# A new stored order for a gated-attention and MLP kernel, and a last result that leaves in thirds

## The chip, the cores and the metric

The kernel runs on one core of a Trainium2 chip. The metric is the device time of one execution in microseconds, lower is better: 575.98 us is the median of three runs, 575.77 to 577.02. Engines are named as in the profile: PE is TensorE, PEld its weight loads, DVE VectorE, ACT ScalarE, POOL GpSimd, SP SyncE, which here issues the DMAs.

## The reference

Gated linear attention with a complex gate over 4 × 8 heads, 768 steps, head dimension 48, and on its output an MLP of width 384 → 2048 → 384 over 3072 tokens:

```python
mag = np.sqrt(a_re * a_re + a_im * a_im)
scale = np.minimum(mag, 0.999) / (mag + 1e-06)
a_re_n, a_im_n = (a_re * scale, a_im * scale)
for t in range(S):
    new_re = ar * S_re - ai * S_im
    new_im = ar * S_im + ai * S_re
    kv = np.einsum('bhd,bhe->bhde', k[:, :, t], v[:, :, t])
    S_re, S_im = (new_re + kv, new_im)
    y[:, :, t] = np.einsum('bhd,bhde->bhe', q[:, :, t], S_re)
...
h = x @ w_in
g = h * (1.0 / (1.0 + np.exp(-1.702 * h)))
return (g @ w_out).astype(np.float32)
```

## The kernel before

**Attention.** The recurrence is turned into masked products. For each unit of 256 steps, VectorE and ScalarE make from the gate `ri` its magnitude and angle: squares (helper L253), their sum (L270), logarithm and exponential (L365, L366, L374 to L377), the scaled gate (L367) and its clipped magnitude (L380), the angle (L385). Scans along time (L390, L406, L424) give running products and running angles; cosine and sine (L443, L444) turn the queries and keys, and the rotated ones are `qr` and `qk` (all tensor products of two operands have the helper's line L270). Five DMAs on SP then lay each of them out by head in `qkh` (L466, L467, L469, the "remap"). Unit 0 is cut into two parts of 128 steps so that TensorE may start early. `attend` computes for each block of 128 steps and half of the heads the scores (L504), their masking (L508, `pm`), the mixing with the values and the state (L529), the transposed keys (L560, in `kz_ps`; evicted to `kt` by ScalarE at L563 or by VectorE at L564) and the state's update (L554, L569, L573). `kz_ps` holds one pair of transposed heads, so the next transposition waits for the eviction.

**MLP.** The weights come as 16 tiles (A0 to A7 of w_in, U0 to U7 of w_out) of 64-bit words from DRAM into one of four `raw` tiles (L286); ScalarE scales the low words (L288), VectorE takes the top words in two steps (L289, L292) and adds the low ones (L295). The first two blocks, of 256 tokens each, use the fp32 tiles as they are; for the five later ones, of 512 tokens, weights, tokens and hidden values are split into a high and a low part (L304, L307 for weights; `gh` and `gl`, L627 and L629). L610 is the hidden product, L619 and L623 the gating function, L643 the projection, L659 the eviction of the three 128×512 result tiles `o`, L664 the result DMA.

**Order.** All of this is added to one plan of 1827 steps with declared reads and writes. `Plan.order` decodes a table of step numbers (`ORDER`) and a set of steps that run on their second engine (`OTHER`), and the steps are then written out in that order under a manual schedule; so each engine's queue, and SP's, is the table's. The durations given with each step were used only to make the table. A table load (L840) is put ahead of each ScalarE function that needs another set of functions. L451 is a row of matmuls without use for the result, put ahead of the first real ones and between them.

Of the kernel before, what the change touches and what calls it, by code (L numbers as in the profile page):

```python
# [105 lines left out]
}  # L106
ORDER = (
    "0D=He00jUK0A&EF0001&0D}O808#*j08s#j08;>m00#h60EhsK00;n80E_@x09F7701*I>09pWD0FVF)09ycF0Eqxx0AT=%09OE!09XKL0Ac`N"
    "0Av9W0AK(L02u&{0B8V?0FwY|0097M0F(f10A>LQ0Brzk00ID&0SN$-0B-<e0SW+a0B``B0C50w0Gj}o0CE8l0Gt4U0CWJD0TKY60GR-F0G<F0"
    "02%;x00RJ@0Cxcs01E(k0HOe(00aRP0C@nT0Sf^P0HFXB02=`f0Hgq>01yDB0H**P0Tloe0T}?Q0H^^L0I~oR0T%#z0UZFd0T=+Z01W{i0DAzn"  # L110
    "0DJ(y0U7|S0JZ@i0IUFg0Ji}k02TnQ0IdMH0UH2*01g1J0J#9L0UQA+03HB;0I>kN0J{LZ0U-e?0Kfnh0LTD<0LcKs0VM$=03!jm0KEXh0U`jt"
    "0LlQv0K@>x0386u0LB3%04)Ka0L%c#0L}o^0M7sy0V)970M-B`02lz;03QG#04M=003`t60Ve@103iU?0VV+0044y}0Neq%03ra{04@PA05SmG"
    "0k;6q04D)40O0`Q04V`405<^M0V@FG0L=k10WJV4051UF0l5G$0lEO~04o8z0OSEP05bu<0W<*R05||S0W|<D0OkRl0lWdg06YOU0PFxd0OtTP"
    "0O$e306_sb0O|ng06PJ}05k!X0P6w50mK0g0mlH*0Pg_q0MY@y0P+Ae0m%Um0Mh_I0Qmqm0lon90muQx0m=c(080VJ0Pq1#07e1+06hTl0QCXR"
    "0YL#d0YU+u0Yd>g0Qdn!06zgY0Y?El0Q3Mu0nY(F0XzWu0Yv~n0Zsu(073yt0nh;U0ZIWz0nz|O0QUjY0nGtR07U^l0Y3rJ0ZakR0agLt0YCu$"
    "0Z#x-0oDOm0Z;+e0RREl0h$3=0RI3;0oVXX0Z{>207(I?0a5{40n`9Z0aE}<0aOA108Rk=0bBu90Q>=60RaL40cipO0onor0b&8!0owut0b>E&"
    "0tf;G0bT)U0hj^?08au30Q~`%0to^P0RjRJ0tEpB0crvY0hs}G0t*5S0bc<G0c8ON0uTXj0b~IN0uKQP0cHVP0ulkL0u%vf0ipsI0c!zZ0p9`i"
    "0;U2H0q6o40pI~_0uupl0bv1c0vQ2z0dN8p0viE!0u}-30vrK)0vZ8#0v`dc0o?(z0e}J^0v-Wz0v!Qz0k8rg0;d9~0doPg0ek|f0eAu<0;&Qe"
    "0qO#)0pS7b0pkL&0pbDf0wMwI0<i()0;~b$0wn?O0rdf!0<Hn@0eJ$l0i6P`0<!|N0e%630qp{{0=5Br0iOc60gM5C0=EHy0p<d_0p|hn0fz#u"
    "0>1+L0fqs80rmpG0igl%0=WVC0ww~y0rLU(0x$vi0fYiE0=of&0x|+80r~<n0{jBO0s8_p0z3iy0yY7S0sR6u0w@890>c5L0fhp@0=)r=0g3|s"  # L120
# [20 lines left out]
    "1+WDq2E+xq2E_!B1u+K31tkT#1?&Yg1d#=<1d;`@1u_LU2FC`-1d|5I1+N9|1-k`31vCY`1vLfl1vUjd2FeD@1vm!G1@Q&+1v&*j1vv%11wRF{"
    "2F(V}1-}LE1x5zX1waMx1v>>u1wjVT1;7RM1;GZ<1w;k*2GRw>1wsWw1yBV^1@i^?1xE(c2Gj-j1-=H=1^NX_1+xW31xp3;1^ES11^fk02G$1G"
    "1^Wir1e66)1xy7~1x*G31;YhZ1_1@M1^ouu1+@m+1-1s;1;z!p1<wUf1zH7G2HXbS1yly!1;qvg1^xxN1zQDN1;+)@1;hnc1y}`N1!V<Y1zrXJ"
    "1<?lI1!M-`2H^$*1z81V1=0m>1z-i!1;_=}1<3_s1z`o$1!)H21=a;)1!o511!xB31#ksy1<D5H1!@Kb2Id881<MBK1<VC;1#$(~1#bn|2IvL`"
    "1#Ja$2I&Us1=$7%1{wwq1_%Xt1`h?z1=<Gd1<nTS1$YJn2JHqA1_=fc1_}le2JQwM1#|}Q1`7u81{4Mi1$G5`1`P%k1{?)-1{MW<1|0?y2Jr?L"
# [869 lines left out]
```

## Time and profile before

| | before |
|---|---|
| median of three runs | 575.98 us |
| profiled execution | 577.74 us, of which the span in the trace 576.0 us |
| mean granted clock of TensorE | 0.993 |
| TensorE matmuls busy | 535.9 us (93%), 6236 matmuls |
| VectorE busy | 453.5 us (79%) |
| ScalarE busy | 312.9 us (54%) |
| SP's DMA queue | 79.09 MB, 50.7% of 16 engines |

TensorE is the busiest engine by the mean, but the mean lies over three stages: a start in which TensorE has hardly work, a long stretch in which it has no idle time, and an end in which the last results leave. Each is to be read apart.

### The profile page before, as it was taken

To read this page: it belongs to the slowest core of one execution; us is meant where nothing else is said; L and a number is where in the kernel's file an instruction comes from. 1 tells how busy PE (TensorE), PEld (TensorE's weight loads), DVE (VectorE), ACT (ScalarE), POOL (GpSimd) and SP (SyncE) were. 2 spreads that over 40 slices of the span, in tenths; PEclk is the share of its full clock that TensorE was granted. 3 is DMA by queue.
4 is the path that set the end of the run, shared out by engine and by line. 5 is a ranking of instruction groups with operands and counts; after the bars stand their busy time and mean duration, and the time that the engine had idled before them with its cause. 6 is when DMAs were issued, how large, how long until landed. Compare 5 with 4: busy or idle time off the path is not lost.

```text
span 576.0 us, 14758 instructions
## 1 busy us (share of the span) xinstructions
PE 535.9 (93%) x6236; PEld 444.4 (77%) x6236; DVE 453.5 (79%) x822; ACT 312.9 (54%) x458; POOL 27.0 (5%) x86
## 2 busy tenths in 40 slices
...
GB/s 302 219 142 292 200 202 308 82 189 100 159 87 193 56 166 145 124 122 166 138 185 69 123 165 180 73 225 92 92 140 57 191 127 85 58 55 56 37 93 66
DMA packets 30902, 80.06 MB, mean 139 GB/s; under 512 B 4208, under 2 KB 7024, under 8 KB 30832
## 3 DMA queue, kind: packets, MB, share of 16 engines
q1 hardware_dynamic: 30832, 79.09, 50.7%
...
q14 instruction: 21, 0.17, 0.1%
HBM read 55.44 MB, written 4.72 MB: 104 GB/s over the span
## 4 chain that ended last, share of the span: by engine, by line
PE 84%; DVE 9%; DMA 2%; ACT 1%; issue 1%; SPq 1%; POOL 0%; DVEq 0%; POOLq 0%
PE o_ps L643 33%; PE h_ps L610 33%; PE x_ps L529 6%; PE p_ps L504 5%; PE kz_ps L560 4%; PE kz_ps L554 2%; DMA raw<-in_w_in_dram 1%; DMA qkh<-qr 1%; DVE valA L292 1%; DVE s L406 1%; DVE pm L508 1%; PE h_ps L451 1%; DVE qr L270 1%; DVE qk L270 1%; DVE valU L295 1%
## 5 line engine op out<-in xcount | busy, mean ns | idle before, releaser
L623 ACT ACTIVATE g<-h_ps 128x512 f32<-128x512 f32 x80 | 46.4, 596 | 121.7 <-PE h_ps L610 85.2
L643 PE MATMUL o_ps<-gh,hiU 128*128 128x512 f32 x240 | 95.7, 399 | 0.0
L610 PE MATMUL h_ps<-xhi,hiA 128*128 128x512 f32 x240 | 95.4, 398 | 0.0
L643 PE MATMUL o_ps<-gl,hiU 128*128 128x512 f32 x240 | 93.7, 391 | 0.0
L610 PE MATMUL h_ps<-xhi,loA 128*128 128x512 f32 x240 | 93.6, 390 | 0.0
L643 PE MATMUL o_ps<-gh,loU 128*128 128x512 f32 x240 | 93.5, 390 | 0.0
L610 PE MATMUL h_ps<-xlo,hiA 128*128 128x512 f32 x240 | 93.4, 389 | 0.0
L840 ACT ACT_TABLE_LOAD x61 | 78.3, 1283 | 1.9 <-PEq L1003 0.8
L627 DVE CAST gh<-g 128x512 fp32r<-128x512 f32 x74 | 31.0, 421 | 42.8 <-PE o_ps L643 26.1
L629 DVE TENSOR_TENSOR gl<-g,gh 128x512 fp32r<-128x512 f32 x80 | 54.6, 684 | 2.4 <-ACT gh L626 0.7
L677 DVE TENSOR_REDUCE fit<-raw_w 128x1 f32<-128x256 f32 x96 | 38.0, 413 | 19.0 <-DMA raw_w<-in_w_out_dram 17.5
L643 PEld LDWEIGHTS o_ps<-gl,hiU 128*128 128x128 f32 x240 | 45.1, 188 | 9.9 <-DVE gl L629 0.4
L610 PEld LDWEIGHTS h_ps<-xhi,loA 128*128 128x128 f32 x240 | 45.1, 188 | 9.6
L643 PEld LDWEIGHTS o_ps<-gh,hiU 128*128 128x128 f32 x240 | 45.1, 188 | 9.1 <-issue 0.4
L610 PEld LDWEIGHTS h_ps<-xlo,hiA 128*128 128x128 f32 x240 | 45.1, 188 | 8.8
L643 PEld LDWEIGHTS o_ps<-gh,loU 128*128 128x128 f32 x240 | 45.1, 188 | 8.7
L610 PEld LDWEIGHTS h_ps<-xhi,hiA 128*128 128x128 f32 x240 | 45.1, 188 | 8.6
L563 ACT ACTIVATE kt<-kz_ps 128x224 f32<-128x224 f32 x66 | 23.3, 353 | 46.1 <-PE kz_ps L560 34.0
L643 PE MATMUL o_ps<-g,valU 128*128 128x256 f32 x192 | 44.8, 380 | 1.7 <-ACT g L619 1.7
L270 DVE TENSOR_TENSOR qk<-qk,s 128x768 f32<-128x768 f32 (+1 forms) x52 | 45.6, 888 | 0.5 <-DMA qk<-in_qk_dram 0.4
L508 DVE TENSOR_TENSOR pm<-p_ps,mask 128x512 f32<-128x512 f32 x48 | 32.8, 683 | 15.1 <-PE p_ps L504 12.3
L610 PE MATMUL h_ps<-x,valA 128*128 128x256 f32 x192 | 44.2, 381 | 0.0
...
## 6 DMA issues: line engine op xcount, KB each, us to landing
...
```

The source lines that it names most:

```text
L270: add(en, t, rank, lambda: e.tensor_tensor(out=out, in0=a, in1=b, op=alu), **kw)
L504: mm(p_ps[to : to + QL, j, lo:L], lhsT=at(h, 1, c)[:, lo : lo + QL], rhs=at(h, 0, c)[:, lo:L], start=True, stop=True)
L508: add("DVE", d_t(CW), rk(4 * c + hh), lambda hh=hh: dve.tensor_tensor(out=pm[hh], in0=p_ps, in1=mask, op=ALU.mult), r=["P"], w=[f"pm{hh}"])
L529: mm(x_ps[32 * j : 32 * j + 32, r, :], lhsT=lt, rhs=rt, start=n == 0, stop=n == len(steps) - 1)
L563: one = ("ACT", a_t(2 * KD) - 0.12, lambda e=e: act(out=kt[0][:, 2 * e : 2 * e + 2, :], in_=k_ps, func=AF.Copy))
L610: mm(h_ps[hb][:, hs], lhsT=ww[:, r * T + f * P : r * T + (f + 1) * P], rhs=x[:, r, :], start=r + k == 0, stop=r == NR - 1 and k == len(ter ...
L623: add("ACT", a_t(N) - 0.15, rk(i + f / 2), lambda hb=hb, hs=hs: act(out=g32[hb][:, hs], in_=h_ps[hb][:, hs], func=AF.Silu, scale=SLOPE), r ...
L627: two = ("DVE", d_t(N, 2), lambda hb=hb, hs=hs: dve.tensor_copy(out=high.g(hb)[:, hs], in_=g32[hb][:, hs]))
L629: add("DVE", d_t(N), rk(i + f / 2), lambda hb=hb, hs=hs: dve.tensor_tensor(out=glo[hb][:, hs], in0=g32[hb][:, hs], in1=high.g(hb)[:, hs].b ...
L643: mm(o_ps[m][:, 0:N], lhsT=y[:, f * DM + m * P : f * DM + (m + 1) * P], rhs=x[:, hs], start=i == 0 and f == 0 and k == 0, stop=i == NP - 1 ...
L677: add("DVE", d_t(CK), rk + 2, lambda x=x, op=op: dve.tensor_reduce(out=f_w[:, x, n : n + 1], in_=weights.looked_at()[:, :, 1], op=op, axis ...
L840: nc.scalar.preload_act_table_set(o[5])
```

## The change

Three things are changed. The table `ORDER` and the set `OTHER` are new. Of the steps with two engines, 34 have changed theirs: of the K evictions ten go to ScalarE (L563) and two to VectorE; of the weight splits three to ScalarE and two to VectorE; single squares, conversions, evictions and lines go either way, and the last of the three final result evictions goes to ScalarE. The table loads on ScalarE are 63 instead of 61; the matmuls are the same 6236.

The durations that the planner was given for a weight load, a load of queries and keys and a load of values are changed; they act only where a table is made. And in the last block the eviction and the DMA of each third no longer depend on the other users of the tile that they write.

```diff
-        add("SP", 1.9 + 1.3 * (n == 0), rk - 4, lambda: dma(out=raw.bitcast(I32), in_=(w_in if m == "A" else w_out)[j].bitcast(I32)),
+        add("SP", 1.9, rk - 4, lambda: dma(out=raw.bitcast(I32), in_=(w_in if m == "A" else w_out)[j].bitcast(I32)),
...
-        add("SP", z * (1.9 if np_ == 2 else 1.0), rk("ldqk"), lambda: dma(
+        add("SP", z * 1.5, rk("ldqk"), lambda: dma(
...
-            add("SP", 0.87, rk(4 * c) - 5, lambda vt=vt, c=c: dma(out=vt, in_=v[u, c]), w=[kv])
+            add("SP", 1.04, rk(4 * c) - 5, lambda vt=vt, c=c: dma(out=vt, in_=v[u, c]), w=[kv])
...
-            either("D", one, two, rk(NP + 0.1), r=[f"o{m}"], w=[f"ob{m}"] + spent)
+            either("A" if final and m == NR - 1 else "D", one, two, rk(NP + 0.1), r=[f"o{m}"], w=[f"ob{m}"] + ([] if final else spent))
         for ms in (((0,), (1,), (2,)) if final else ((0, 1, 2),)):
             add("SP", len(ms) * N * P * 4 / 410e3, rk(NP + 0.1), lambda ms=ms: dma(
                 out=to[:, ms[0] : ms[-1] + 1, :], in_=high.o(n)[:, ms[0] : ms[-1] + 1, 0:N]
-            ), r=[f"ob{m}" for m in ms] + spent)
+            ), r=[f"ob{m}" for m in ms] + ([] if final else spent))
```

The first rows in which VectorE's queue differs, at the start of the program, before (`valA` is a weight tile, `s` are the gate's factors, `ri` the gate):

```order
L270 TENSOR_TENSOR s_80<-s_80,s_81 128x3x128 x2
L289 TENSOR_SCALAR valA_149<-raw_72 128x768
L367 SCALAR_TENSOR_TENSOR s_81<-ri,s_80 128x3x128
L292 SCALAR_TENSOR_TENSOR valA_149<-raw_72,valA_149 128x768
L367 SCALAR_TENSOR_TENSOR s_81<-ri,s_80 128x3x128
L289 TENSOR_SCALAR valA_160<-raw_74 128x768
L380 TENSOR_SCALAR s_80<-s_80 128x3x128 x2
```

and in the changed kernel:

```order
L270 TENSOR_TENSOR s_80<-s_80,s_81 128x3x128 x2
L367 SCALAR_TENSOR_TENSOR s_81<-ri,s_80 128x3x128
L380 TENSOR_SCALAR s_80<-s_80 128x3x128
L289 TENSOR_SCALAR valA_152<-raw_72 128x768
L367 SCALAR_TENSOR_TENSOR s_81<-ri,s_80 128x3x128
L292 SCALAR_TENSOR_TENSOR valA_152<-raw_72,valA_152 128x768
L380 TENSOR_SCALAR s_80<-s_80 128x3x128
L295 ISA valA_152<-raw_72,valA_152 128x1536
```

One scaled gate and one clipped magnitude now stand ahead of the first step that needs a weight tile. Further down the same queue, the rows that stand ahead of the first rotated queries (`qr`), before:

```order
L289 TENSOR_SCALAR valA_208<-raw_71 128x768
L270 TENSOR_TENSOR qr<-qk,s_80 128x3x128 x2
L424 SCALAR_TENSOR_TENSOR s_85<-small,s_81 128x128 x3
L270 TENSOR_TENSOR qk<-qk,s_85 128x3x128
L406 SCALAR_TENSOR_TENSOR s_84<-s_80,small,s_82 128x128 x3
```

and in the changed kernel:

```order
L289 TENSOR_SCALAR valA_207<-raw_74 128x768
L437 TENSOR_SCALAR small<-s_85 128x3
L398 TENSOR_SCALAR small<-s_83 128x3
L399 RECIPROCAL small<-small 128x3
L424 SCALAR_TENSOR_TENSOR s_85<-small,s_81 128x128 x3
L406 SCALAR_TENSOR_TENSOR s_84<-s_80,small,s_82 128x128 x3
L270 TENSOR_TENSOR qr<-qk,s_80 128x3x128 x2
```

The scans of part 1 (L424, L406) stand ahead of the queries of part 0 instead of behind them. ScalarE's queue at the first evictions of K (`kt`), before:

```order
L365 ACTIVATE s_82<-s_82,small 128x3x256
L288 ACTIVATE raw_74<-raw_74 128x768
L366 ACTIVATE s_82<-s_82 128x3x256
L376 ACTIVATE s_83<-s_82,small 128x3x256
L374 ACTIVATE s_81<-s_81,small 128x3x256
L563 ACTIVATE kt_97<-kz_ps 128x224
```

and in the changed kernel:

```order
L365 ACTIVATE s_82<-s_82,small 128x3x256
L366 ACTIVATE s_82<-s_82 128x3x256
L376 ACTIVATE s_83<-s_82,small 128x3x256
L563 ACTIVATE kt_97<-kz_ps 128x224 x2
L288 ACTIVATE raw_74<-raw_74 128x768
```

The first two evictions stand ahead of L374, which needs VectorE's L367. The end of SP's queue, as a difference (`o` holds the last results, the names behind "waits" are the engines waited for):

```order
 L695 DMA raw_w<-in_a_dram 128x256 [waits DMAHW2_49,DVE_49]
-L664 DMA out_dram<-o_5701 128x512 [waits DVE_49]
-L664 DMA out_dram<-o_5701 128x512 x2
+L664 DMA out_dram<-o_5703 128x512 [waits DVE_49] x2
+L664 DMA out_dram<-o_5703 128x512 [waits Activation_49]
 L843 TENSOR_LOAD count [waits DVE_49]
```

Before, the first of the three DMAs waited for VectorE's last eviction and the other two for nothing more; now each waits for its own. Of the early loads on SP, the weight tile A6 is issued two U tiles earlier.

## Rows read from the trace of the kernel before

**Rows 1.** Busy us (and instructions) by stretches; then granted clock, DMA share, GB/s.

```profile
8.50:25.00 16.50, 0.00 (x0) 0.00 (x0) 16.33 (x42) 10.92 (x20) 1.51 (x4) 1.00 0.75 278
25.00:36.40 11.40, 5.97 (x48) 4.52 (x48) 11.29 (x19) 10.20 (x15) 3.43 (x5) 0.95 0.61 147
36.40:51.50 15.10, 14.41 (x312) 10.48 (x313) 13.44 (x24) 9.42 (x15) 0.77 (x5) 0.81 0.54 163
51.50:96.00 44.50, 42.25 (x429) 36.09 (x429) 42.35 (x63) 36.60 (x54) 2.75 (x7) 1.00 0.88 267
96.00:240.00 144.00, 143.89 (x1942) 121.84 (x1941) 131.69 (x217) 107.45 (x151) 5.69 (x20) 1.00 0.52 130
240.00:560.00 320.00, 319.95 (x3467) 264.37 (x3466) 227.40 (x436) 131.49 (x195) 6.89 (x25) 1.00 0.45 115
```

**Rows 2.** TensorE's waits: what waited for what, total us, times, longest.

```profile
PE h_ps L451 <- DMA qkh<-qr: 25.1, 1, 25.1
PE kz_ps L560 <- ACT kt L563: 5.7, 2, 5.3
PE o_ps L643 <- ACT g L619: 1.7, 1, 1.7
```

**Rows 3.** Timeline of TensorE: start, duration, line, idle before and its releaser.

```profile
25.14 4.49 PE L451 MATMUL h_ps<-qk,ident 128*128 128x256 f32 x12 [25.14 <-DMA qkh<-qr]
29.56 0.76 PE L504 MATMUL p_ps<-qkh 128*32 128x128 f32 x32
...
36.43 0.64 PE L560 MATMUL kz_ps<-ident,qkh 112*128 112x112 f32 x2 [5.32 <-ACT kt L563]
...
51.50 0.70 PE L610 MATMUL h_ps<-x,valA 128*128 128x256 f32 x2
```

**Rows 4.** Timeline of ScalarE, 31 to 36.5 us.

```profile
31.48 0.90 ACT L288 ACTIVATE raw<-raw 128x768 int32<-128x768 uint32 x1
...
33.21 0.94 ACT L376 ACTIVATE s<-s,small 128x768 f32<-128x768 f32 x1
35.20 0.94 ACT L374 ACTIVATE s<-s,small 128x768 f32<-128x768 f32 x1 [1.06 <-DVE s L367]
36.04 0.34 ACT L563 ACTIVATE kt<-kz_ps 128x224 f32<-128x224 f32 x1
```

**Rows 5.** Timeline of VectorE, 8 to 71 us.

```profile
8.57 0.56 DVE L289 TENSOR_SCALAR valA<-raw 128x768 int32<-128x768 int32 x1 [1.92 <-DMA raw<-in_w_in_dram]
9.04 0.55 DVE L367 SCALAR_TENSOR_TENSOR s<-ri,s 128x384 f32<-128x384 f32 x1
...
11.32 0.74 DVE L380 TENSOR_SCALAR s<-s 128x384 f32<-128x384 f32 x2
...
20.24 0.55 DVE L289 TENSOR_SCALAR valA<-raw 128x768 int32<-128x768 int32 x1
20.71 1.14 DVE L270 TENSOR_TENSOR qr<-qk,s 128x384 f32<-128x384 f32 x2
21.77 1.23 DVE L424 TENSOR_TENSOR_SCAN s<-small,s 128x128 f32<-128x128 f32 x3
...
23.37 1.23 DVE L406 TENSOR_TENSOR_SCAN s<-s,small,s 128x128 f32<-128x128 f32 x3
...
39.74 0.39 DVE L573 COPY st<-kz_ps 128x224 f32<-128x224 f32 x1 [0.78 <-PE kz_ps L554]
...
70.29 0.56 DVE L289 TENSOR_SCALAR valA<-raw 128x768 int32<-128x768 int32 x1 [2.06 <-DMA raw<-in_w_in_dram]
```

**Rows 6.** Groups of ScalarE: busy us, mean ns of one, idle before.

```profile
L840 ACT ACT_TABLE_LOAD x61 | 78.3, 1283 | 1.9 <-PEq L1003 0.8
L623 ACT ACTIVATE g<-h_ps 128x512 f32<-128x512 f32 x80 | 46.4, 596 | 121.7 <-PE h_ps L610 85.2
L563 ACT ACTIVATE kt<-kz_ps 128x224 f32<-128x224 f32 x66 | 23.3, 353 | 46.1 <-PE kz_ps L560 34.0
```

**Rows 7.** Timeline at the end, and the result DMAs (L664) by their line.

```profile
569.34 0.69 DVE L659 TENSOR_SCALAR o<-o_ps 128x512 f32<-128x512 f32 x1 [0.69 <-PE o_ps L643]
...
570.06 1.31 SPq L664 DMA_DIRECT2D out_dram<-o  x3
...
L664 SPq DMA_DIRECT2D out_dram<-o x3: 343/426/447, 570.1 to 570.9; - x3
...
DMA to landing us min/median/max: 2.1/2.8/3.7
```

More of the change, by code (lines that the diff above doesn't have):

```diff
@@ L102 @@
 OTHER = {
[3 rows of a table removed]
+    260, 262, 403, 420, 430, 434, 436, 440, 449, 486, 511, 512, 558, 561, 585, 591, 600, 610, 617, 647,
+    650, 657, 660, 670, 675, 680, 727, 738, 749, 760, 765, 775, 789, 792, 812, 821, 834, 932, 949, 1006,
+    1016,
 }
 ORDER = (
[L108 to L110 removed]
@@ L111 @@
[L111 to L120, printed above, removed]
@@ L141 @@
[L141 to L145, printed above, removed]
+    "0D=He00jUF0A&D|0E7U80EGZi0EPfk0EYlm0E+;K08{{v0961709F8500saE09pWD00{tF0Eqxx0A2uL0E_?`0F3~@01N<%0FD5V01p6S09OE$"
@@ new lines @@
+    "000130I2|90Av7Q0FeM_0T2LZ0BHal0FnS^02%;l01E&S0BZo00Biu70SEwY0SN$Y0F?li0Gj}C0B-=80C51E0GR-u0CE5U0CNEn01W_i0TBS5"
+    "01^Oo0D%CX0TTeA0CoVO0Cxct0HOe;0C)hS0Am3P00ID{0TlqI0Sf>F0H*;N0IC2E0I~q90C@nj0TuwX0H^?Z0JQ+D01yBK0JZ@g0Js2q0IdMI"
+    "0U7|h02}~(0J{Jl0DS=$022VN0IvZX0I&eJ03!e$0LTFx0UiMi0Db`>0K5Re0XP830T=+v02Bbh0V4p*0I>kQ0UrR&0Kx$x0k#1k0KNdu04)H2"
+    "0K)*!0K@<!0Vn{)0LB2&0LK6&0Du4=03ZO=0VMz?03iU?0M-F10VDv}0M`H&0N?-?0k;4r0MP*10V)7D02cwc0NMb}0W1I*0NViE03rY=0Nw$)"
+    "05SmG04@P5051UI0O0{A0WAS00lEO^0WbjU0WSeD0lNS&0WtvJ0lxvf0OkPc0673O0OSBM0WJXJ0W<(O0PO%e0PX=b05bs60W$z80P_GU0O$cW"
@@ new lines @@
+    "0lfgz04o6U06PHX05t)=0l)w(0QdpH06_u606YLT0O|q60Sy5T0mT8r0S^G{0mlKx0m}iL0sa9w07d~p0XG530Pq1#0YU-D0Pg`h080VR0Yd>h"
+    "0Q3Pw0Qvz(0m=bI0Qmt(0nY$K0Pz6z0XzUg07L<p0Z9Qp06qaq0Zsv)0nh<H06hUe0Y(5t0n!0W0agG%0RI730j2@X0sjF006+o&0nq_Z0QLbu"
+    "0ZakY0n7nd0a5_~0oDOo0Z;+d07wDX0a^i?0Z{>50QUja07n6q07(JZ0aF110aO8907?M+0bT+D0aXC}08Ih{0onm+0tErv0s{eK0oedd0t5lv"
+    "0cZjU08Ro40b&7{0bc?J0Q~?@0tW&L0RjQu0uBLN0uKQL0i*&90b~Lf0u2HS0bl|Y0p9|q0R#c)0c8Ph0uTY|0c!!Q0dE0n0R;jQ0uccQ0qO!1"
+    "0vG`Y0d)cE0rUZ&0qy~20vQ4t0u}*h0dN8v0pJ020vrKh0u=(N0c-*v0dWEy0v-Y&0c`<x0o?+p0wDq-0dfI%0;vIj0ht1-0pS9x0qg<d0<Zz&"
@@ new lines @@
+    "0wV$S0<i()0;~cg0p$WE0q+5#0<r<{0<Hmb0h<Bw0<;3J0eS(l0<{9O0qp_i0eb?r0ek_f0rmlS0<8g^0f7O60jL4z0x$vc0eu3u0r>(Z0rLU("
+    "0x<%-0=NP)0{a1s0y6>l0=fZt0j>d`0r~>D0yF}@0w)3c0yY9X0e%9&0yhEt0yP1!0sR4n0igoB0yqJO0yzPH0w@B(0x1EB0=@x*0!9M-0fYj>"
+    "0f++q0xAMJ0>lEs0{#Lk0zCpp0=)r_0xSY80>uJI0?z_I0{;Pp0xkkc0>=T00xtr{0{{X$0zU%<0zm>m0!jk`0zv{q0ki`H0iyy;0gD1e0>%Rd"
+    "0gVDh0?7fT0gwTw0gnR*0|^360#gG70?Gpl0|)~R0#X830?Pvr0}BGo0!{+W0g(b!0}cZW0|EkE0g?f!0h0n)0#yQ50$l=61DFC{0h9tu0hI$3"
+    "0$KwR0}ukx0#E|k0_6f<0%ihH0$Bpu0~G>b0~P|?0$T!T0jmR<1DXRE0%QXj1DgV20j&aJ0}=zA0&oJ+0}}#g0^9;)1DyjG0%-%D1EK=o0?q>6"
@@ new lines @@
+    "0&4=&0%`(f0^S1C0^kFm0~!IZ1E2zN1ET`r0@MO>0^$N}0@VU-0_Fpz0^<VK1E&J-0@ng=0`LPH1Ed2S0(AqW1EB(M104e(10Dgf0^|aE0kZ;j"
+    "0&@a%0(%1I0(=9g0(S!O0)ztC0`dc?1F8ae10Msd10e&e10n)>0(}Fq0_XyM0`mj10)_(h1MC8V0ks150)GPO273du0`~&y0`vo}1GEC`0{8>1"
+    "0_+0$10@4G11<x#111860)PWA27Cjz0)YaD27LnU0*(fL0*L~M10(|{126+90)qoF1MUL)1F!?O1Fr&)0*V780+0fW0`3De1M>qi0+RzN1MLQX"
+    "11bYG13LzQ1Gxr)11kgX1G)n?0*nK=1MmYZ1G@w90+<4k1M&m*27&`O27?3l0*wPa12Y5q2805V12_XM0-6Io1HA+E0+s_g13m-w0+|Ao1N;J&"
+    "1H1!20-Xau1NZ|$1Nj5K1N#D(1HS`80-FOv0-Oeg14RO!28ILv1N{bv0-yq)1Hc3T1O)_@14IM@0-*y&14#o;14;w`1O@{~0-^&?14{y<28aTr"
@@ new lines @@
+    "14skG15*Zx1Ih#k15gHv155+U1OWq01Ox+71PKGo16c%@1I+}M1HuFd15yK628#n!28;%c1JDAc1I`211H%K+16l)C1H=Rh1egR1162f>17ZVP"
+    "1Pum`1P%lP1eycV16KoF1JeV~17rq|1Plg{17HJP1P=pV178E+1Jnb>29X2T1K|Xp1e^oL1IGlL1L6Z?17!rD1P}w`29g8F17QRa29pD417-vg"
+    "1QP?;18f7;1fv9@1f&F_1g8Vp18xK41f2us18M_k1gQp;1IYxQ19k&%1Lp>n1KI|b1f>IQ18D@_1f~OU1giwD19$`#18W0u1g`_=19t=E19AiD"
+    "19JqZ2A2bL2ABk@2AKpO1KR|!1m6S}19=171hNC_1Kk8519}7@2ATta1M37A1R?~p2Ac%n2Al(X19b!51gr$%1hE7o1mXjH1Q-UL1A+u41g!&p"
+    "1APXb1SSNu1QZ6J1hxZ#1S<oB1K$MY1SbQ31BC;G1SkaK1Q`Ui1R4Y+1S|%i1n30h1RDe#2B8Gz1iA*I1SteH1RVsv1i1r<1iJ+11ndMh1iS?4"
```

36 lines of the change are left out of this document (14 added, 22 removed), and 3 rows, old and new, of the table OTHER.

## The prediction

> **What bounds the kernel now.** I read first the busy time by stretches, with the stretches cut where TensorE's behaviour changes [rows 1]. From 96 us to 560 us TensorE is busy 143.89 of 144.00 and 319.95 of 320.00 us: whatever the new order does there, it can take out 0.16 us at most, and it can put waits in. From 8.5 to 96 us VectorE is the full engine (16.33 of 16.50, 11.29 of 11.40, 13.44 of 15.10, 42.35 of 44.50), and TensorE does little before 36.4 (5.97 us, most of it the twelve warming matmuls, 4.49 us [rows 3]). So there are three stages: a prelude in which VectorE makes the first factors, masks and weight tiles; a body that is TensorE and nothing else; a tail after the last projection. An order can only win in the first and the last.
>
> The waits of TensorE confirm it: after the start there is one long one, 5.3 us for a ScalarE eviction of the transposed K (`kt`, L563), and a 1.7 us one for `g` (L619) [rows 2]. The first is seen from three engines. TensorE's first scores run at 29.56, and its second K transposition only at 36.43 [rows 3]. ScalarE reaches the eviction at 36.04, because it sits in its queue behind L374, which had waited 1.06 us for VectorE's L367, although L376 ahead of that was done by 34.15 [rows 4]. And TensorE then runs at a granted clock of 0.81 of full speed from 36.4 to 51.5, against 1.00 later [rows 1]: part of that stretch was at 1.2 GHz instead of 2.4, and 15.10 × 0.19 = 2.9 us went there.
>
> **The prelude, from VectorE's side.** Its idle time is 1.92 us ahead of the first weight tile at 8.57 [rows 5], and inside the four stretches 0.17 + 0.11 + 1.66 + 2.15 = 4.1 us [rows 1]. All of it together, 6.0 us, is the ceiling of what the new order can win there with the same work. Three parts of it are touched.
>
> First, the 1.92 us. VectorE waited at 8.57 for the first weight load. In the new order one L367 (0.55 us) and one of the two L380 of 0.74 us together (about 0.4 us) stand ahead of that wait, and both need only squares and scales made before; they fill 0.95 us of the gap. Worth −0.95.
>
> Second, the 2.06 us at 70.29, again a wait for a weight tile (A6) [rows 5]. Its load is now issued two loads of U tiles earlier on SP, so it should have landed; −2.06. The loads that fall behind it in return are those of U tiles, which are converted one to three tiles later.
>
> Third, the 1.66 us between 36.4 and 51.5, the largest of them 0.78 us for the state product (L554) [rows 5], which itself came late because K was. With the eviction moved ahead of L374, it goes in large part. I take −1.6 for it and for the scraps beside it, and give 0.65 us back for a sine on ScalarE (L444 of unit 1's first part) behind which VectorE's rotations now stand closer: that stall does not exist in the trace, its bounds are 0 and the 2.06 of the longest wait that VectorE has after 9 us, and 0.65 is my estimate from adding up the durations ahead of the two in both queues. So −0.95 − 2.06 − 1.6 + 0.65 = **−4.0 us**.
>
> Against it stands one step. The queries of part 0 (`qr`, L270, 20.71 to 21.85) now come behind one more L289 (0.55 us) and the three scans each of L424 and L406 of part 1 (1.23 us each) that stood behind it [rows 5]: 3.0 us less 0.95 already won, some 2 us later. The remap DMAs of `qkh` go out with it, and the first scores move from 29.56 to about 31.4. The queue of SP behind them is the later remaps and one load; nothing on TensorE needs either before 36.
>
> **The prelude, from TensorE's side.** The eviction stands right behind L376 and no longer behind L374. ScalarE's chain ahead of L376 loses one weight tile's low words (L288, 0.90 us [rows 4]), and by my adding up of the durations in VectorE's new queue it starts about as much later; so L376 ends again near 34.3, the eviction runs then, and TensorE goes on near 34.7 instead of 36.43: −1.7. If the wait is then some 2 us and not 5.3, the clock may stay at full speed, up to −2.9 more. The idle time that is left, 15.10 − 14.41 and 44.50 − 42.25, is 2.9 us [rows 1], a part of which is VectorE's two stalls seen from here. This ledger allows −1.7 to −7.5; VectorE's says −4.0, and the smaller gain holds, because every hidden block of the first MLP unit waits for VectorE's tiles. Bounds of the prelude: 0 (all of it swallowed by the later `qr`) and −6.0 (the ceiling).
>
> **The body.** The matmuls are the same in number and shape, so only waits can come. Ten evictions of K (353 ns each) and three weight splits go from VectorE to ScalarE, two of each come back, and ScalarE gets two more table loads (1283 ns) [rows 6]: some 3.0 + 2.6 us of work more on an engine that is busy 107.45 of 144.00 us from 96 to 240 us, and 131.49 of 320.00 after [rows 1]. In sum that is hidden by the 36 us of slack; in place it may not be, since an eviction now stands behind whatever ScalarE does. The nearest row is a TensorE wait on ScalarE of 1.7 us [rows 2]; I take half of one, **+0.8**, with bounds 0 and two and a half of them, +4.2. The planner's changed durations for loads act on nothing here: the stored table sets the order.
>
> **The tail.** The last projection ends TensorE's work at 569.3. Before, the third eviction on VectorE ran 569.34 to 570.03, and all three result DMAs waited for it: issued from 570.06 to 570.92, the last took 3.7 us to land (574.6), and the span ended 1.4 us later [rows 7]. Now each DMA waits only for its own third, and the last eviction is on ScalarE, idle there: 596 ns for the same shape by the mean of L623 [rows 6], so done at 569.95, one DMA issued at once. The first of the three DMAs before had nothing in front of it and took 2.1 us [rows 7]; the third one will now be in that position, its brothers having gone out near 567.8 and 568.7. So it lands near 572.1 instead of 574.6: −2.5, of which I take **−2.4**, since the count's load, which came behind the DMAs, now comes behind them by as much. Bounds: −0.9 if it still takes 3.7 us, −2.6 if ScalarE's eviction is a little quicker than VectorE's. The Trainium skill, page "DMA: Bandwidth & Descriptors", section on the anatomy of one DMA, fits about 2.0 us fixed plus the bytes over 436 KB per us, for another issuing path; by it the 256 KB would take an estimated 2.6 us, the tail would give 1.9, and the sum would be 0.5 us higher. The row is shorter, and the row is used.
>
> **Sum.** −4.0 + 0.8 − 2.4 = −5.6 us. The profiled execution took 577.74 us, 1.76 above the median of 575.98, with a span of 576.0; the sum is one of differences and is carried to the median: 575.98 − 5.6 = **570.4 us** (profiled 572.1, span 570.4).
>
> **The rivals.** *B: the clock falls again.* TensorE's wait near 33 us stays long enough, or comes at another place of the first 50 us, and real matmuls run at 1.2 GHz as they did before. What speaks for it is that the later `qr` gives TensorE less to do until 31; against it, that the wait shrinks. The prelude then gains only the resumption, −1.7: 575.98 − 1.7 + 0.8 − 2.4 = 572.7. The page "TensorE: Matmul & The Clock Gate" of the Trainium skill, Part 1, says that throttled is the default state and that recent activity releases it; the row of 0.81 behind a 5.3 us wait agrees, and by it any new wait of that size brings the half clock back.
>
> *D: the prelude gains nothing.* The scores start 1.8 us later, and the remap of the keys, which follows, ends the wait in place of the eviction; VectorE's won time turns into waiting for TensorE's products. Then only the tail is left: 575.98 − 2.4 = 573.6, up to 574.6 with some of the body's waits.
>
> *C: evictions on ScalarE stall the body (slower).* ScalarE takes its queue in order, and ten evictions in the units between 100 and 230 us now stand among Ln, Exp and table loads. The row shows what one such place costs when it goes wrong: 5.3 us [rows 2]. One of them gives 575.98 − 6.4 + 5.3 = 574.9, within a hair of no change; two give 580.2. It decides from 6.4 + 1.15 = 7.6 us of new waits. Against it: ScalarE has a quarter of that stretch free, and TensorE has matmuls of the MLP between attention steps to hide a late eviction behind; for it, there is no wait at all there now, so any misfit shows in full.
>
> **How the numbers follow.** What a measurement of this kernel can tell from no change is about 0.2%, 1.15 us. Chances: the forecast 0.55 (568.6 to 572.0); better, the ceiling of the prelude with a wait-free body, 575.98 − 6.0 − 2.6 = 567.4, 0.06; B 0.13; D 0.12; C 0.14, of which 0.06 end within 0.2% and 0.08 above. Faster: 0.55 + 0.06 + 0.13 + 0.12 = 0.86; same 0.06; slower 0.08. The range 567.2 to 574.6 leaves out C and the ends of the others, a little under 0.2.
>
> **What would show it.** Tail: three result DMAs issued about a microsecond apart, the last near 0.7 us behind the last projection and landing 2.1 us later. Prelude: VectorE idle about 1 us ahead of the first weight tile and not at all for A6; first scores near 31.4; the 5.3 us wait cut to 2 or so; the granted clock above 0.95 between 36 and 51; the first hidden block (L610, 51.50 [rows 3]) near 47.5. Body: TensorE's waits after 96 us below 1 us in sum. Wrong would be waits of TensorE on `kt` after 96 us, a first hidden block later than 50, or a last DMA that still takes 3.7 us.

## The result: 569.7 us, and the profile after

The changed kernel takes 569.69 us (median of six runs, 568.97 to 570.73). The kernel before, on the same chip, takes 577.11 us (six runs, 575.77 to 579.22). The ratio is 0.9864, with a 95% interval of 0.9842 to 0.9887: 7.8 us less, 6.5 to 9.1. The two profiled spans are 576.0 and 568.6 us, 7.4 us apart, and the ledgers below (sums of where the time went) are made with these two.

The busy time by stretches (stretch and its length, then PE, PEld, DVE, ACT, POOL with instruction counts, granted clock, DMA share, GB/s), to be read beside [rows 1]:

```profile
8.50:25.00 16.50, 0.00 (x0) 0.00 (x0) 16.17 (x42) 12.44 (x23) 0.19 (x1) 1.00 0.80 304
25.00:36.40 11.40, 10.34 (x122) 7.57 (x123) 11.23 (x19) 9.57 (x15) 2.38 (x5) 1.00 0.50 126
36.40:51.50 15.10, 13.42 (x263) 10.68 (x263) 14.87 (x26) 12.04 (x20) 1.16 (x6) 1.00 0.84 318
51.50:96.00 44.50, 43.92 (x553) 37.23 (x552) 43.86 (x65) 39.91 (x62) 2.42 (x8) 1.00 0.72 223
96.00:240.00 144.00, 143.27 (x1933) 120.34 (x1932) 130.56 (x214) 108.56 (x152) 6.10 (x22) 1.00 0.52 129
240.00:552.00 312.00, 311.64 (x3317) 257.75 (x3316) 222.33 (x427) 125.63 (x187) 5.43 (x23) 1.00 0.45 116
```

In the three stretches from 25 to 96 us TensorE's idle time has fallen from 5.43 + 0.69 + 2.25 = 8.37 us to 1.06 + 1.68 + 0.58 = 3.32 us, and the granted clock is 1.00 in all of them, where it had been 0.95, 0.81 and 1.00. Behind 96 us there was 0.16 us of idle time; now there are 0.73 + 0.36 = 1.09 us. TensorE's waits, to be read beside [rows 2]:

```profile
PE h_ps L451 <- DMA qkh<-qr: 25.9, 1, 25.9
PE kz_ps L554 <- DVE st L573: 1.2, 1, 1.2
PE p_ps L504 <- DMA qkh<-qk: 0.5, 1, 0.5
PE kz_ps L560 <- POOL s L383: 0.5, 1, 0.5
PE kz_ps L560 <- ACT kt L563: 0.4, 1, 0.4
PE kz_ps L554 <- DMA v<-in_v_dram: 0.3, 1, 0.3
```

The 5.3 us wait for `kt` has gone: the second transposition of K (L560) runs at 32.48, right behind the matmuls ahead of it. The 0.4 us that is still listed for `kt` stands at 79.02; the kernel before has one like it in the 5.7 us of its two waits [rows 2]. The 1.7 us wait for `g` has gone. The timeline of TensorE, beside [rows 3]:

```profile
25.86 4.61 PE L451 MATMUL h_ps<-qk,ident 128*128 128x256 f32 x10 [25.86 <-DMA qkh<-qr]
30.39 1.30 PE L504 MATMUL p_ps<-qkh 128*32 128x128 f32 x32
...
32.48 0.41 PE L560 MATMUL kz_ps<-ident,qkh 112*128 112x112 f32 x2
...
46.77 2.86 PE L610 MATMUL h_ps<-x,valA 128*128 128x256 f32 x12
...
79.02 0.41 PE L560 MATMUL kz_ps<-ident,qkh 112*128 112x112 f32 x2 [0.43 <-ACT kt L563]
```

The first scores are 0.8 us later, the first hidden block (L610) is 4.7 us earlier. ScalarE's part in that, beside [rows 4]: the eviction follows L376 at 32.07, and L374 comes 4.5 us behind it.

```profile
31.18 0.94 ACT L376 ACTIVATE s<-s,small 128x768 f32<-128x768 f32 x1
32.07 0.36 ACT L563 ACTIVATE kt<-kz_ps 128x224 f32<-128x224 f32 x1
...
36.55 0.94 ACT L374 ACTIVATE s<-s,small 128x768 f32<-128x768 f32 x1
```

VectorE's timeline ahead of the first weight tile, beside [rows 5]: L289 waits for nothing any more. Ahead of it, the second sum of squares (L270) now waits 1.10 us for ScalarE, where it waited 0.35 before; VectorE's idle time in the first 8.5 us fell from 4.28 to 3.26 us.

```profile
6.64 0.56 DVE L270 TENSOR_TENSOR s<-s,s 128x384 f32<-128x384 f32 x1 [1.10 <-ACT s L253]
7.12 0.55 DVE L367 SCALAR_TENSOR_TENSOR s<-ri,s 128x384 f32<-128x384 f32 x1
7.78 0.43 DVE L380 TENSOR_SCALAR s<-s 128x384 f32<-128x384 f32 x1
8.12 0.55 DVE L289 TENSOR_SCALAR valA<-raw 128x768 int32<-128x768 int32 x1
```

Tile A6, for which VectorE had waited at 70.29 [rows 5], is issued on SP at 52.38:

```profile
52.38 0.33 SPq L286 DMA_DIRECT2D raw<-in_w_in_dram  x1
```

The end of the timeline, beside [rows 7]: the last eviction is ScalarE's, and the three DMAs stretch over 2.54 us instead of 1.31.

```profile
562.83 2.54 SPq L664 DMA_DIRECT2D out_dram<-o  x3
...
564.41 0.60 ACT L658 ACTIVATE o<-o_ps 128x512 f32<-128x512 f32 x1 [6.21 <-PE o_ps L643]
```

The same three by their line, L664, from issue to landing:

```profile
DMA to landing us min/median/max: 2.0/2.0/2.1
```

**The ledger.** The last projection frees its result at 564.41 instead of 569.34, 4.93 us earlier. What follows takes 568.6 − 564.4 = 4.2 us instead of 6.66, 2.47 less. Of the 4.93, idle time from 25 to 96 us gives 5.05 (8.37 − 3.32, the later start included), TensorE's busy time 0.8 (535.9 to 535.1 us for the same 6236 matmuls), and the body takes 0.93 back. The 0.8 us is a net figure: the experiment on the clock below takes it apart.

### The profile page after: what moved, and what is told of

It reads as the page before. It is cut to its first block, busy times and chain, and to the rows that moved or that the text cites. A ratio compares the mean times of both kernels' runs of the same rounds, so it can differ in the third digit from the quotient of the medians.

```text
span 568.6 us, 14760 instructions
## 1 busy us (share of the span) xinstructions
PE 535.1 (94%) x6236; PEld 443.2 (78%) x6236; DVE 450.8 (79%) x816; ACT 315.4 (55%) x466; POOL 24.1 (4%) x86
## 4 chain that ended last, share of the span: by engine, by line
PE 77%; DVE 8%; DMA 6%; ACT 6%; issue 1%; SPq 1%; POOL 0%; ACTq 0%; DVEq 0%; POOLq 0%
PE o_ps L643 31%; PE h_ps L610 30%; PE x_ps L529 6%; PE p_ps L504 4%; PE kz_ps L560 3%; PE kz_ps L554 2%; DMA qkh<-qk 2%; DMA ri<-in_a_dram 2%; DMA v<-in_v_dram 1%; DVE qk L270 1%; ACT L840 1%; DMA qkh<-qr 1%; DVE s L270 1%; DVE s L424 1%; DVE pm L508 1%
## 5 line engine op out<-in xcount | busy, mean ns | idle before, releaser
L643 PE MATMUL o_ps<-gh,hiU 128*128 128x512 f32 x240 | 95.8, 399 | 0.0
L610 PE MATMUL h_ps<-xhi,hiA 128*128 128x512 f32 x240 | 95.7, 399 | 0.0
L643 PE MATMUL o_ps<-gl,hiU 128*128 128x512 f32 x240 | 93.7, 391 | 0.0
L610 PE MATMUL h_ps<-xhi,loA 128*128 128x512 f32 x240 | 93.6, 390 | 0.0
L643 PE MATMUL o_ps<-gh,loU 128*128 128x512 f32 x240 | 93.5, 390 | 0.0
L610 PE MATMUL h_ps<-xlo,hiA 128*128 128x512 f32 x240 | 93.5, 389 | 0.0
L563 ACT ACTIVATE kt<-kz_ps 128x224 f32<-128x224 f32 x74 | 26.1, 353 | 56.3 <-PE kz_ps L560 38.6
L643 PEld LDWEIGHTS o_ps<-gl,hiU 128*128 128x128 f32 x240 | 45.0, 188 | 9.9 <-DVE gl L629 0.4
L610 PEld LDWEIGHTS h_ps<-xhi,loA 128*128 128x128 f32 x240 | 45.1, 188 | 9.5
L643 PEld LDWEIGHTS o_ps<-gh,hiU 128*128 128x128 f32 x240 | 45.1, 188 | 9.1 <-ACT s L261 0.2
L610 PEld LDWEIGHTS h_ps<-xlo,hiA 128*128 128x128 f32 x240 | 45.2, 188 | 8.7
L643 PEld LDWEIGHTS o_ps<-gh,loU 128*128 128x128 f32 x240 | 45.1, 188 | 8.6
L610 PEld LDWEIGHTS h_ps<-xhi,hiA 128*128 128x128 f32 x240 | 45.1, 188 | 8.6
L270 DVE TENSOR_TENSOR qk<-qk,s 128x768 f32<-128x768 f32 (+1 forms) x52 | 45.7, 889 | 0.8 <-ACT s L444 0.5
L643 PE MATMUL o_ps<-g,valU 128*128 128x256 f32 x192 | 45.8, 380 | 0.0
L610 PE MATMUL h_ps<-x,valA 128*128 128x256 f32 x192 | 45.4, 382 | 0.1
```

The costliest lines, as they stand in the source:

```text
L270: add(en, t, rank, lambda: e.tensor_tensor(out=out, in0=a, in1=b, op=alu), **kw)
L563: one = ("ACT", a_t(2 * KD) - 0.12, lambda e=e: act(out=kt[0][:, 2 * e : 2 * e + 2, :], in_=k_ps, func=AF.Copy))
L610: mm(h_ps[hb][:, hs], lhsT=ww[:, r * T + f * P : r * T + (f + 1) * P], rhs=x[:, r, :], start=r + k == 0, stop=r == NR - 1 and k == len(ter ...
L643: mm(o_ps[m][:, 0:N], lhsT=y[:, f * DM + m * P : f * DM + (m + 1) * P], rhs=x[:, hs], start=i == 0 and f == 0 and k == 0, stop=i == NP - 1 ...
```

## The experiments

Gains are ratios to the runs of the kernel before on the same chip, turned into us of 577, with their 95% interval. One execution is a poor witness here: the kernel before took 574.2 to 580.3 us in the 72 executions made for comparison, on three chips, and its mean granted clock went with the time: 578.6 us in the median of the 22 executions at 0.988, 576.7 of the 6 at 0.995. The changed kernel was at 0.998 to 1.000 in all of its six.

### The tail alone

The final lines of the diff in the old order, with the three DMAs in the order of their evictions.

> The old order with the new tail alone: the third result eviction on ScalarE, each of the three DMAs waiting for its own eviction, the three in the order of their evictions. My theory: the last DMA has nothing in front of it and lands 2.1 us after its issue, so 2.4 us less than before, with nothing changed up to the last projection. Rival: the last DMA takes as long as it took behind two others (3.7 us), and 0.9 us is left of it.

Measured: 2.8 us less (1.4 to 4.0). Its result DMAs land as in the changed kernel:

```profile
DMA to landing us min/median/max: 2.0/2.0/2.3
```

So the last DMA's 3.7 us was the queue behind its two brothers, and the tail's term stands. The timeline of VectorE in this run shows how much one gap depends on the execution: the start of the program is the same as before, and VectorE waited 0.71 us for the first weight tile where [rows 5] has 1.92.

```profile
7.36 0.56 DVE L289 TENSOR_SCALAR valA<-raw 128x768 int32<-128x768 int32 x1 [0.71 <-DMA raw<-in_w_in_dram]
```

### One wait removed in the old order

ScalarE's queue:

```diff
 L376 ACTIVATE s_83<-s_82,small 128x3x256
-L374 ACTIVATE s_81<-s_81,small 128x3x256
-L563 ACTIVATE kt_97<-kz_ps 128x224
-L375 ACTIVATE s_81<-s_81 128x3x256
-L563 ACTIVATE kt_97<-kz_ps 128x224
+L563 ACTIVATE kt_97<-kz_ps 128x224 x2
+L374 ACTIVATE s_81<-s_81,small 128x3x256
+L375 ACTIVATE s_81<-s_81 128x3x256
```

> The old order with one change on ScalarE: the first two evictions of transposed K (L563) ahead of L374 and L375. Theory V (VectorE sets the prelude): the 5.3 us wait of TensorE shrinks, but only VectorE's 1.66 us of idle time between 36 and 51 us can be won, so at most 1.6 us. Theory T (TensorE's wait and its half clock set the prelude): TensorE goes on near 34.5 instead of 36.43 and the granted clock stays up, 1.9 to 4.8 us.

Measured: 1.3 us less (0.2 to 2.3): theory V's bound fits, and the lower end of theory T is not excluded. TensorE's timeline shows what came in place of the wait:

```profile
33.28 0.64 PE L560 MATMUL kz_ps<-ident,qkh 112*128 112x112 f32 x2 [2.22 <-ACT kt L563]
...
37.00 1.06 PE L504 MATMUL p_ps<-qkh 128*32 128x128 f32 x32 [0.56 <-DVE pm L508]
...
50.49 0.51 PE L554 MATMUL kz_ps<-v,kt 128*32 128x48 f32 x13 [2.35 <-issue]
```

The wait for `kt` fell to 2.2 us, and the next scores then waited for the mask of the first ones, which stands on VectorE behind weight steps. The longest gap that came instead, 2.35 us in the middle of a row of L554, has no releaser in the profile ("issue" is time in which the engine waited for nothing that is recorded); its cause is open. The stretches show that the clock still fell:

```profile
25.00:36.40 11.40, 9.18 (x85) 6.37 (x83) 11.29 (x17) 10.52 (x16) 3.53 (x6) 0.86 0.71 161
36.40:51.50 15.10, 11.17 (x279) 8.46 (x276) 14.87 (x25) 7.80 (x13) 0.67 (x4) 0.95 0.70 244
```

### VectorE's two gaps filled in the old order

```diff
+L367 SCALAR_TENSOR_TENSOR s_81<-ri,s_80 128x3x128
+L380 TENSOR_SCALAR s_80<-s_80 128x3x128
 L289 TENSOR_SCALAR valA<-raw_72 128x768
...
-L289 TENSOR_SCALAR valA<-raw_74 128x768
 L295 ISA valU<-raw_71,valU 128x1536
 L367 SCALAR_TENSOR_TENSOR s_81<-ri,s_83 128x3x256
+L289 TENSOR_SCALAR valA<-raw_74 128x768
```

> The old order with two changes on VectorE: one L367 and one L380 stand ahead of the first step that needs a weight tile, and the first step on tile A6 stands two steps later (behind an L295 and an L367). Both fill gaps in which VectorE waited for a weight load, 0.95 and about 1.9 us. Theory V: 2.9 us less. Theory T: TensorE's wait for K is still there and ends 0.95 us earlier, by VectorE's L367; the second gap is hidden; so 1 us less.

Measured: 1.2 us less (−0.1 to 2.4). Theory T's 1 us fits; theory V's 2.9 lies outside.

### Both together

> Both of the former: the evictions of K ahead of L374, and VectorE's two gaps filled. Theory V: the parts add, 4.5 us less. Theory T: 2.9 to 5.8 us less, and the gaps are worth 1 us of it whether or not the evictions are moved.

Measured: 1.4 us less (0.8 to 2.1), less than either theory said. TensorE's waits, where one of 5.3 us had been:

```profile
PE o_ps L643 <- ACT g L619: 2.7, 1, 2.7
PE p_ps L504 <- DVE pm L508: 2.5, 2, 2.0
PE kz_ps L560 <- ACT kt L563: 2.5, 1, 2.5
```

The wait for `g` is a wait for tile A6 seen through ScalarE, whose timeline has L288 of that tile ahead of the gating function:

```profile
68.65 0.94 ACT L288 ACTIVATE raw<-raw 128x768 int32<-128x768 uint32 x1 [2.93 <-DMA raw<-in_w_in_dram]
```

VectorE's freed time was no gain for TensorE; it turned into waiting, of VectorE too: its idle time from 51.5 to 96 us is 4.38 us here and was 2.15 before. Theory V fell with that. For theory T too the sum is too small, unless the waits that came instead are counted.

### The loads

SP's queue (tile A4 ahead of U2 and of unit 1's queries and keys, A6 ahead of U3 and U4); on VectorE, A4's three steps also stand ahead of U2's:

```diff
-L286 DMA raw_73<-in_w_out_dram 128x1536
-L412 DMA qk<-in_qk_dram 128x3x512
 L286 DMA raw_74<-in_w_in_dram 128x1536
-L360 DMA ri<-in_a_dram 128x1536
-L286 DMA raw_72<-in_w_in_dram 128x1536
+L286 DMA raw_73<-in_w_out_dram 128x1536
+L412 DMA qk<-in_qk_dram 128x3x512
+L360 DMA ri<-in_a_dram 128x1536
+L286 DMA raw_72<-in_w_in_dram 128x1536
+L286 DMA raw_74<-in_w_in_dram 128x1536
 L286 DMA raw_71<-in_w_out_dram 128x1536
 L286 DMA raw_73<-in_w_out_dram 128x1536
-L286 DMA raw_74<-in_w_in_dram 128x1536
```

> The old order with one more idea alone: weight tile A4's load ahead of U2's and of the load of unit 1's queries and keys on SP, A4's conversion ahead of U2's on VectorE, and so A6's load (same buffer as A4) ahead of U3's and U4's. Theory L (the prelude ends when the weight tiles arrive): A6 was issued at 61.7, took 8.5 us and held up VectorE for 2.06, ScalarE for 1.94 and through it TensorE for 1.7 us; issued near 54 it lands before they need it, and 1.7 to 2.1 us go. Theory D (the DMA engines are full there, share 0.88, so what comes earlier pushes another load back): nothing, within 0.5 us.

Measured: 0.5 us more (−0.9 to 1.9). ScalarE no longer waited for A6, but twice (1.96 and 0.92 us) for U tiles (w_out) that now came later:

```profile
62.57 0.94 ACT L288 ACTIVATE raw<-raw 128x768 int32<-128x768 uint32 x1 [1.96 <-DMA raw<-in_w_out_dram]
```

That is theory D's outcome: a tile moved forward in a nearly full stretch moves another one back.

### All three hand edits together

> The old order with the three hand edits together: K evictions ahead of L374, VectorE's two gaps filled, A4's and A6's loads early. Theory L: the two former edits gave 1.4 us together because TensorE then waited 2.7 us for the gating function behind A6's load; with that load early this wait goes too, 4 us less than before. Theory D: 1.4 us less, as without the loads.

Measured: 0.8 us less (−0.5 to 2.0); theory D again. The profiled execution is the slowest of the ten (580.78 us). In it TensorE's wait for `g`, which theory L saw gone, is the longest of all runs, because ScalarE waited for U tiles ahead of it, and the granted clock was low in all three stretches (0.84, 0.78 and 0.96):

```profile
PE o_ps L643 <- ACT g L619: 4.0, 1, 4.0
```

### One wait put back into the changed kernel

```diff
 L376 ACTIVATE s_83<-s_82,small 128x3x256
+L374 ACTIVATE s_81<-s_81,small 128x3x256
 L563 ACTIVATE kt_97<-kz_ps 128x224 x2
...
-L374 ACTIVATE s_81<-s_81,small 128x3x256
 L261 ACTIVATE s_83<-s_83 128x3x256
```

> The changed kernel with L374 of unit 1 put back ahead of the first two evictions of K, so that they wait again for VectorE's L367 (33.35 to 34.30): the first eviction moves from 32.07 to about 35. Theory T (TensorE's first wait sets the prelude): 2.5 to 3 us more, and more if the clock falls to half. Theory V/L (VectorE and the loads set it): less than 1 us more, for VectorE goes on with weight tiles meanwhile.

Measured: 573.62 us, 0.9928 of the kernel before (0.9902 to 0.9954), where the changed kernel is 0.9864: some 3.7 us of the gain went, with an uncertainty of about 2. The mechanism of [rows 4], brought back by this one move, in ScalarE's timeline:

```profile
34.44 0.94 ACT L374 ACTIVATE s<-s,small 128x768 f32<-128x768 f32 x1 [2.22 <-DVE s L367]
35.29 0.34 ACT L563 ACTIVATE kt<-kz_ps 128x224 f32<-128x224 f32 x1
```

in TensorE's:

```profile
35.68 0.64 PE L560 MATMUL kz_ps<-ident,qkh 112*128 112x112 f32 x2 [3.31 <-ACT kt L563]
```

and in the stretch behind it, where the granted clock fell from 1.00 to 0.84:

```profile
36.40:51.50 15.10, 14.15 (x317) 10.79 (x317) 11.69 (x21) 9.37 (x16) 1.16 (x6) 0.84 0.74 265
```

In the ledger TensorE's idle time from 25 to 96 us is 4.28 + 0.95 + 0.58 = 5.81 us instead of 3.32, 2.5 more, and its busy time 536.7 us instead of 535.1, 1.6 more. Theory T's forecast holds here, with the clock as a second part of the price; theory V/L's, under 1 us, does not. But VectorE did not go on with weight tiles: its idle time from 8.5 to 96 us rose from 1.37 to 4.74 us, 3.2 of it in waits for TensorE's scores. So this run shows what the wait costs, and not which of the two engines sets the time.

### The K evictions back on VectorE

The ten evictions of units 1 to 5 run as L564 instead of L563, at the same places of the new order.

> The changed kernel with the ten evictions of K that went to ScalarE (units 1 to 5) put back on VectorE, in the new order. If the body has slack on both engines, as the forecast assumed, within 0.5 us of the changed kernel; if the move to ScalarE was needed in this order, TensorE waits for VectorE in the units between 100 and 230 us, 1 to 5 us more.

Measured: 570.46 us, 0.9880 of the kernel before (0.9847 to 0.9914), 0.9 us above the changed kernel's ratio and not to be told from it. TensorE then waits for VectorE where it had not:

```profile
PE kz_ps L560 <- DVE kt L564: 0.9, 1, 0.9
```

The evictions on ScalarE cost nothing that shows.

### The new prelude before the old body

The new table's first 414 steps, up to the last matmul of the first MLP block, then all other steps in the old order on the old engines, and the new tail.

> The new order up to the last matmul of the first MLP block (about 110 us), the old order and the old engines behind it, and the new tail. If the gain is made of prelude and tail, and the new body costs 0.9 us of TensorE's idle time behind 96 us against 0.16 in the old order, as the ledger of idle time says, this is as fast as the changed kernel or up to 0.9 us faster. If the new body order is needed to keep the prelude's lead, 1 us slower or more.

Measured: 572.35 us, 4.3 us less than before (2.9 to 5.7), 1.6 us more than the tail alone gives and some 3.5 us short of the changed kernel. That is the second outcome named, the new body is needed, but the seam has a wait of its own, which the whole new order does not have:

```profile
PE h_ps L610 <- ACT g L619: 2.6, 1, 2.6
```

Without these 2.6 us the prelude would by this estimate be worth some 4.2 us. I have no version that beats the changed kernel.

### The old prelude before the new body

The counterpart, with the new tail: the old table's first 412 steps, then the rest in the new order.

> The counterpart: the old order up to the last matmul of the first MLP block, the new order and engines behind it, and the new tail. If prelude, body and tail stand by themselves: the tail's gain alone, less up to 0.9 us, so 1.6 to 2.8 us less than before. If the new body helps, more than 3.5 us less.

Measured: the time of the kernel before, 0.0 us (−1.4 to 1.4), though the tail is the new one. The body's idle time explains 0.9 us of it (TensorE busy 142.99 of 144 us, 143.89 in [rows 1]):

```profile
96.00:240.00 144.00, 142.99 (x1961) 119.88 (x1964) 133.33 (x218) 108.24 (x156) 5.83 (x19) 1.00 0.51 129
```

The rest is up to 1.9 us, with an uncertainty of about 2. In the profiled execution it stands in TensorE's busy time, 538.6 us against 535.9: the clock was low in the first stretches again, and behind a wait for `g` it fell once more (0.83 from 70 to 80 us). Twelve projections (L643) then took 4.54 us, where the same twelve took 2.86 in the kernel before:

```profile
74.00 4.54 PE L643 MATMUL o_ps<-g,valU 128*128 128x256 f32 x12 [1.98 <-ACT g L619]
```

Whether the other nine executions lost it in the same way is not shown. What follows is that the new body by itself brings no gain, and that the parts do not stand by themselves: the tail, the new prelude before the old body and the new body behind the old prelude would add up to 2.8 + 1.6 − 2.8 = 1.6 us, and the whole table gives 7.8. The wait at the seam is 2.6 us of that difference.

### The next link of the chain

The evictions as above, and on VectorE the first mask ahead of L367, the state's copy and the second mask ahead of a weight step:

```diff
+L508 TENSOR_TENSOR pm_95<-p_ps,mask 128x512
 L367 SCALAR_TENSOR_TENSOR s_81<-ri,s_82 128x3x256
 L295 ISA valA_160<-raw_74,valA_160 128x1536
 L380 TENSOR_SCALAR s_82<-s_82 128x3x256
+L573 COPY st_94<-kz_ps 128x224
+L508 TENSOR_TENSOR pm_96<-p_ps,mask 128x512
 L292 SCALAR_TENSOR_TENSOR valU_246<-raw_73,valU_246 128x768
-L508 TENSOR_TENSOR pm_95<-p_ps,mask 128x512
...
-L573 COPY st_94<-kz_ps 128x224
...
-L508 TENSOR_TENSOR pm_96<-p_ps,mask 128x512
```

> The old order with the first two evictions of K ahead of L374, and also the first two maskings (L508) and the state's copy (L573) moved ahead on VectorE: the first mask ahead of L367, the second ahead of a weight step. When the evictions alone were moved, TensorE's wait was followed by one for the mask, and idle time between 30 and 52 us stayed at 6.2 us. If TensorE's chain of waits sets the prelude, that idle time now falls to about 3 us and the time by 2.5 to 4 us. If VectorE's work is what counts, nothing is won beyond the 1.3 us of the evictions alone, for its work is the same.

Measured: 0.2 us less (−1.0 to 1.4), so not the 2.5 to 4 us. The expectation had a gap in it: of the 6.2 us of idle time it started from, 2.35 were the gap without a releaser, which no mask could take out. Three waits for `kt` (4.1 us in sum) and one for a later mask filled the place:

```profile
PE kz_ps L560 <- ACT kt L563: 4.1, 3, 3.0
PE p_ps L504 <- DVE pm L508: 1.0, 1, 1.0
```

The second theory's bound holds in the number, but not its reason: TensorE did wait, only at other places.

### The clock by itself

Ten more warming matmuls (each is two instructions in the profile) in the old order between the first and the second transposition of K.

> The old order with ten more warming matmuls (L451) between the first two transpositions of K, where TensorE waited 5.3 us, so that the wait stays and TensorE doesn't rest in it. The granted clock between 36 and 52 us should be near 1.00 instead of 0.81. If the half clock costs what the granted clock says, 2.9 us less. If the small matmuls there hardly run slower at half clock, as TensorE's busy time says (it is 0.8 us less in the changed kernel), at most 0.8 us less.

Measured: 0.9 us less (−0.3 to 2.1), with the clock at 1.00 in the first two stretches, where it had been 0.95 and 0.81; the second of them:

```profile
36.40:51.50 15.10, 14.08 (x321) 10.98 (x322) 14.87 (x26) 9.82 (x16) 0.67 (x4) 1.00 0.69 240
```

In the time of the kernel that is near the smaller of the two prices, and 2.9 us lies outside. But the smaller price was not read from the same matmuls: TensorE's busy time in the changed kernel belongs to another order. Here the order is the old one, so the same matmuls can be laid side by side, from the second transposition of K to the third. In the kernel before:

```profile
36.43:42.30 5.87, 5.87 (x80) 4.03 (x81) 4.88 (x9) 4.63 (x6) 0.21 (x2) 0.51 0.56 130
...
36.86 1.94 PE L451 MATMUL h_ps<-qk,ident 128*128 128x256 f32 x4
...
39.37 1.35 PE L504 MATMUL p_ps<-qkh 128*32 128x128 f32 x32
```

and with the wait filled:

```profile
35.08:38.78 3.70, 3.70 (x80) 2.60 (x81) 3.70 (x7) 3.67 (x5) 0.10 (x1) 1.00 0.62 165
...
35.33 1.04 PE L451 MATMUL h_ps<-qk,ident 128*128 128x256 f32 x4
...
36.80 1.06 PE L504 MATMUL p_ps<-qkh 128*32 128x128 f32 x32
```

The same 80 matmul instructions, without a gap in either run, take 5.87 us at a granted clock of 0.51 and 3.70 us at 1.00: the half clock cost 2.2 us of TensorE's time, most of the 2.9 read from the granted clock. Only part of it reached the time of the kernel: 0.9 us in the median of ten executions, at most 2.1. The changed kernel's 0.8 us of busy time is smaller because its matmuls take longer elsewhere, about half of it at the start: from the first warming matmul to the first transposition 5.77 us (25.86 to 31.63) against 5.11 before (25.14 to 30.25).

## Why the prediction was right, step by step

**The time and the gain.** The forecast of 570.4 us lies 0.7 from the measured 569.7, and part of that is luck: the gain was forecast at 5.6 us and measured at 7.8 (6.5 to 9.1). The sum started from 575.98, the median of three runs; six runs give 577.11, so 1.1 us of the missing gain was hidden in the start.

**The stages** were read rightly: the gain lies in prelude and tail, and the body only takes.

**The tail**, −2.4: measured 2.47 in the two profiles and 2.8 (1.4 to 4.0) alone. The mechanism, a last DMA with nothing in front of it, is shown by its landing after 2.0 to 2.1 us. The Trainium skill's fit for another issuing path (page "DMA: Bandwidth & Descriptors", anatomy of one DMA) gives an estimated 2.6 us for these 256 KB; these rows, 2.0 to 2.1 us, differ from it as the row of before did.

**The body**, +0.8: measured +0.93, and the size is right by luck. I had priced a wait on ScalarE. The named waits behind 96 us are one of 0.5 us for a remap of keys and one of 0.3 for values, the rest smaller scraps. The K evictions on ScalarE, rival C, are cleared by the run that put them back.

**The prelude**, −4.0: here the term was mis-sized. It measures −5.9 in the ledger (5.05 of idle time and 0.8 of busy time), at the ceiling of 6.0 that I had set. The choice that failed is that of the two ledgers "the smaller gain holds". I took VectorE's idle time for the currency and let TensorE's waits be worth no more. In its own currency the sum was right: VectorE's idle time up to 96 us fell from 8.37 to 4.63 us, 3.7 less where 4.0 was forecast. The time fell by more, because TensorE's waits and the half clock went too; the other ledger, TensorE's, had room for it (−1.7 to −7.5). The runs also speak against adding up gaps one by one: VectorE's gaps filled by hand gave 1.2 us and not 2.9, and with the evictions moved too 1.4 and not 4.5, because VectorE's time came back as waiting. One wait of TensorE put back into the new order cost 3.7 us, though it took no work from any engine; VectorE stood idle 3.4 us longer with it. That in an order in which TensorE hardly waits VectorE hardly waits either is what these traces have in common; that one is the reason of the other is argued, not shown.

Of the single steps, the gap ahead of the first weight tile is filled as forecast, but its 1.92 us was one execution's landing time. The seven traces with that start have 0.71 to 1.92 us, three of them less than 0.95, so there the term is worth less than it was priced. The stall behind the sine (L444), priced at 0.65 us, came with 0.5. The late tile A6 was forecast as a stall of VectorE; it was that, and through ScalarE's queue also the wait of TensorE for `g`. The first scores came 0.8 us later and not 1.8, and the eviction of K ran at 32.1 and not 34.3: ScalarE's chain ahead of it started earlier than my adding up of VectorE's queue said.

**The clock**, rival B: it stayed at 1.00, as the forecast held more likely. My 2.9 us for the half clock was somewhat too much for TensorE's time, 2.2 for the same matmuls in the same order, and too much for the kernel's, of which filling the wait gave 0.9 (−0.3 to 2.1). When the wait was put back, the clock fell and busy time rose by 1.6 us, which is B's mechanism. The Trainium skill, page "TensorE: Matmul & The Clock Gate", Part 1, says that recent activity releases the clock; these runs agree, with 0.84 behind a wait of 3.3 us and 1.00 where the wait was filled.

**Rival D**, the prelude swallowed, did not come true for the whole new order. It did for the hand edits of the old one: a wait was removed and another one took its place, first the mask, then `g`, then a U tile.

What is not settled is which moves of the new table are needed together. The waits removed by hand, alone and together, won at most 1.4 us; the table removed them all at once, and its two halves, tried apart, do not add up to the whole.
